# Attention decode with a gated MLP on one core: cross-partition maxima moved to VectorE, paired V accumulators, and output rows as one 512-column product plus a shared remainder

## The chip, the core and the metric

The kernel runs on one core of a Trainium2 chip. The metric is the time of one execution on the device in microseconds (us). The profile is one execution recorded by the hardware. TensorE (PE) multiplies matrices; its weight loads have rows of their own (PEld). VectorE (DVE) does elementwise work and reductions, ScalarE (ACT) does activations and copies, GpSimd (POOL) does elementwise work, and SyncE (SP) issues nearly all large transfers, which one hardware queue carries out in the order of their issue. SBUF is the on-chip memory with 128 partitions, PSUM the accumulators that PE writes. All data are float32, and PE makes two passes for each product, so a product counts twice in the PE rows of a profile. "Order" below means the list of instructions of one engine as the built program holds it; it has no times. PEclk is the share of its full speed that PE was granted.

## The reference

```python
g = sigmoid((x * gate_w).sum(-1))                    # x: [2, 1, 576]
q = x @ wq                                           # [2, 32 heads, 128]
s = q . k_cache * 128**-0.5                          # 2 x 32 heads x 4096 keys
o = softmax(s) @ v_cache                             # [2, 32, 128]
a = o.reshape(2, 1, 4096) @ wo                       # wo: [4096, 576]
h = gelu(x @ w1 + b1)                                # w1: [576, 4608]
b = h @ w2 + b2                                      # w2: [4608, 576]
out = g * a + (1 - g) * b                            # [2, 1, 576]
```

K and V hold 134 MB each (2 x 32 x 4096 x 128 float32); the four weight matrices hold 9.4, 10.6, 10.6 and 9.4 MB (wq, w1, w2, wo). Each is read once.

## The kernel before

**The ring.** Most of SBUF is one tile `ring` with three slots of 64 KB a partition. A slot takes the K or the V of four heads (a unit: 8.39 MB). There are 16 units, so the stream is K0, V0, K1, V1, up to K15, V15, preceded by `wq` and `w1` and followed by three loads named `last` (table `LAST`, line 66): rows 0 to 28 of w2 in the slot of V14, the rest of w2 and wo rows 0 to 16 in the slot of K15, wo rows 16 to 32 in the slot of V15. `load_next` (line 200) issues the next load on SP when the slot's last reader is done: DVE for a K, PE for a V. The last row of wo comes in three pieces, 288, 144 and 144 columns, so that the end has little left to do.

**The start.** The small inputs come over ACT's queue. `xT` (line 273) holds the transposed inputs. `proj` (line 290) makes q and the hidden layer of the MLP from wq and w1, with products that write 32 output partitions each, four side by side. The gate `zps` is a sum of five products (line 281). `q_unit` (line 345) spreads the q of four units over all partitions (tile `q`, two buffers).

**The loop over the units (line 584).** For unit i, `mul` (DVE, line 508) multiplies K in place by q; `red` adds halves on POOL (line 512) and reduces on DVE (lines 513 and 514); `max_p` takes the maximum in each partition; `max_t` turns it with a PE product against the scaled identity `idsc` into PSUM (line 523); `max_n` reduces that on DVE (line 527) in the next turn, before `softmax` (four exponentials on ACT, line 533). `av` (line 540) does 32 products of 512 columns for the unit before, again four side by side on partitions 0, 32, 64 and 96 of a PSUM tile; `keep` (DVE, line 556) masks the tile and `combine` (PE, line 562) adds it into `oall`, once a unit.

**The end (line 604 on).** PE works through the rows of w2 and wo. A row is 576 columns of 128 partitions, and `acc_mm` (line 365) makes two products of 288 columns from it, each with two output partitions; `acc` holds four such groups at partitions 0, 32, 64 and 96, so two rows go side by side. Half of w2's row 35 lies in SBUF as 16 partitions of eight rows (`wx`, function `mlp_x`), read by four small transfers. Rows 0 to 23 of w2 stand ahead of the last `av`; the remaining rows fill the gaps of `norm_sum`, `norm_t` and `o_turn`, which bring the attention output into the layout `oP`. `wo_out(0, FOLD)` adds wo rows 0 to 22. `last_out` (line 445) copies `acc` on ACT, takes wo rows 23 to 31 as four products of 144 columns each (`part`), folds the copied sums in after row 26, and copies the result out in two halves.

The order of each engine is the order in which the code is written (`manual_schedule`).

## Time and profile before

| | before |
|---|---|
| time, median of 3 runs | 721.58 us (721.48 to 721.66) |
| the profiled execution, first to last instruction (span) | 719.80 us |
| difference between the median and the span | 1.78 us |
| mean granted PE clock | 0.663 |
| PE busy | 237.2 us (33%) |
| DVE busy | 516.8 us (72%) |
| transfer engines: share of the span that the queue q1 carried | 99.2% |
| read from memory | 308.59 MB, 429 GB/s |

The profile lists the times of the three runs, but none of its own execution beside its span; the 1.78 us between the two lie outside the first and the last instruction. In rows of the trace in order of time, the first number is the start in us, the second the duration, then come the engine, the line, the operation, out<-in with the shape, the count, and in brackets how long the engine had stood idle and for whom.

### The profile page before, as it was taken

To read this page: it belongs to the slowest core of one execution; us is meant where nothing else is said; L and a number is where in the kernel's file an instruction comes from. 1 tells how busy PE (TensorE), PEld (TensorE's weight loads), DVE (VectorE), ACT (ScalarE), POOL (GpSimd) and SP (SyncE) were. 2 spreads that over 40 slices of the span, in tenths; PEclk is the share of its full clock that TensorE was granted. 3 is DMA by queue.
4 is the path that set the end of the run, shared out by engine and by line. 5 is a ranking of instruction groups with operands and counts; after the bars stand their busy time and mean duration, and the time that the engine had idled before them with its cause. 6 is when DMAs were issued, how large, how long until landed. Compare 5 with 4: busy or idle time off the path is not lost.

```text
span 719.8 us, 3981 instructions
## 1 busy us (share of the span) xinstructions
PE 237.2 (33%) x1695; PEld 72.1 (10%) x1695; DVE 516.8 (72%) x146; ACT 38.3 (5%) x143; POOL 143.8 (20%) x31
## 2 busy tenths in 40 slices
...
GB/s 409 412 443 431 433 441 419 455 416 448 426 444 427 426 438 430 437 430 441 434 433 433 437 427 437 426 437 434 441 430 444 427 437 422 433 441 431 418 425 307
DMA packets 7277, 308.84 MB, mean 429 GB/s; under 512 B 830, under 2 KB 1362, under 8 KB 1628
## 3 DMA queue, kind: packets, MB, share of 16 engines
q1 hardware_dynamic: 7204, 308.55, 99.2%
...
q10 hardware_dynamic: 56, 0.05, 0.0%
...
HBM read 308.59 MB, written 0.00 MB: 429 GB/s over the span
## 4 chain that ended last, share of the span: by engine, by line
DMA 46%; DVE 35%; PE 16%; issue 1%; ACT 1%; ACTq 0%; POOL 0%; DVEq 0%; SPq 0%; POOLq 0%
DMA ring<-in_A_k_cache_dram 41%; DVE ring L508 19%; DVE s L513 10%; PE av L544 8%; DVE s L514 5%; DMA ring<-in_A_wo_dram 3%; DMA ring<-in_gate_w_dram 3%; PE hps L305 2%; PE qps L305 2%; PE oall L562 1%; PE acc L369 1%; PE mt L523 1%; ACT p L533 1%; ACTq L218 0%; DVE m L518 0%
## 5 line engine op out<-in xcount | busy, mean ns | idle before, releaser
L508 DVE TENSOR_TENSOR ring<-ring,q 128x16384 f32<-128x16384 f32 x16 | 275.6, 17225 | 108.9 <-DMA ring<-in_A_k_cache_dram 108.9
L512 POOL TENSOR_TENSOR ring<-ring 128x3968 f32<-128x3968 f32 x16 | 137.0, 8564 | 494.3 <-DVE ring L508 494.3
L513 DVE TENSOR_REDUCE s<-ring 128x66 f32<-128x8448 f32 x16 | 143.2, 8953 | 1.3
L544 PE MATMUL av<-ring,p 128*32 128x512 f32 x1024 | 133.7, 681 | 11.5 <-ACT p L533 6.2
L523 PE MATMUL mt<-idsc,m 128*128 128x128 f32 x32 | 12.6, 498 | 367.5 <-DVE m L518 367.5
L514 DVE TENSOR_REDUCE s<-ring 128x62 f32<-128x3968 f32 x16 | 68.4, 4276 | 0.0
L533 ACT ACTIVATE p<-s,bs 32x128 f32<-32x128 f32 x64 | 25.5, 398 | 487.8 <-DVE bs L527 486.6
L544 PEld LDWEIGHTS av<-ring,p 128*32 128x32 f32 x1024 | 35.6, 124 | 119.3 <-issue 102.4
L523 PEld LDWEIGHTS mt<-idsc,m 128*128 128x128 f32 x32 | 8.0, 310 | 383.2 <-DVE m L518 289.1
L353 PE MATMUL qb<-qm,spread 64*128 64x512 f32 x8 | 8.3, 1138 | 71.2 <-POOL qm L349 71.2
L562 PE MATMUL oall<-avs,pick 128*64 128x512 f32 x32 | 30.6, 1059 | 0.8 <-DVE avs L556 0.8
L556 DVE TENSOR_TENSOR avs<-av,selr 128x512 f32<-128x512 f32 x16 | 10.9, 680 | 16.1 <-PE av L544 16.1
L392 DVE TENSOR_TENSOR ring<-hps,ring 128x384 f32<-128x384 f32 x3 | 1.7, 558 | 27.2 <-PE hps L305 27.0
...
L349 POOL TENSOR_TENSOR qm<-qall,mine 64x512 f32<-64x512 f32 x4 | 4.1, 1032 | 38.4 <-ACT qall L332 38.4
L533 ACT ACTIVATION_READ_ACCUMULATOR p<-s,bs 32x1 f32 x64 | 11.8, 184 | 0.0
L369 PE MATMUL acc<-ring,hg 128*2 128x288 f32 x142 | 11.6, 456 | 0.0
L305 PE MATMUL hps<-ring 128*32 128x384 f32 x120 | 11.5, 549 | 0.0
L305 PE MATMUL qps<-ring 128*32 128x512 f32 x80 | 11.4, 737 | 0.0
L353 PEld LDWEIGHTS qb<-qm,spread 64*128 64x128 f32 x8 | 2.0, 307 | 74.2 <-POOL qm L349 74.2
L479 DVE COPY ring<-res 2x144 f32<-2x144 f32 x1 | 0.3, 298 | 12.6 <-PE res L483 12.6
L272 PE MATMUL xps<-ident,ring 3*128 3x3 f32 x10 | 1.3, 250 | 23.1 <-DMA ring<-in_gate_w_dram 23.1
...
## 6 DMA issues: line engine op xcount, KB each, us to landing
...
```

Of the source, the lines that this page charges most:

```text
L305: nc.tensor.matmul(ps[32 * j:32 * j + 32, :width], lhs, ts[c][:, o:o + width], start=(k == 0), stop=last, skip_group_check=True,)
L353: nc.tensor.matmul(ps, spread, t.rearrange("p u d -> p (u d)"), start=True, stop=True)
L369: nc.tensor.matmul(acc[o:o + m], lhsT, rhs[:, (s - lo) * DS:(s - lo + 1) * DS], start=start, stop=stop, skip_group_check=True)
L508: nc.vector.tensor_mul(kt[i], kt[i], qs[i].unsqueeze(1).to_broadcast([P, R, DH]))
L512: nc.gpsimd.tensor_add(t[:, :, :DH2], t[:, :, :DH2], t[:, :, DH2:])
L513: nc.vector.tensor_reduce(st[i][:, HALVED:], kt[i][:, HALVED:], AX.X, ALU.add)
L514: nc.vector.tensor_reduce(st[i][:, :HALVED], t[:, :, :DH2], AX.X, ALU.add)
L523: nc.tensor.matmul(mt[i], mx[i].to_broadcast([P, P]), idsc, start=True, stop=True)
L533: nc.scalar.activation(p[w, :, e * RB:(e + 1) * RB], st[i][w].rearrange("p (t c) -> p t c", c=RB), AF.Exp, bias=bias[i][w, e:e + 1], scale ...
L544: nc.tensor.matmul(ps[32 * j:32 * j + 32], p[:, EB * t:EB * t + 32], vt[i][:, RB * t:RB * (t + 1)].rearrange("p r d -> p (r d)"), start=(t ...
L556: nc.vector.tensor_mul(t, avs[i].rearrange("p (r d) -> p r d", d=DH), selr.unsqueeze(2).to_broadcast([P, RB, DH]))
L562: nc.tensor.matmul(oall, pick[:, NO - E - i * E:2 * NO - E - i * E], avs[i].rearrange("p r d -> p (r d)"), start=(i == 0), stop=(i == N - ...
```

## The change

1. **Maxima.** `max_t` becomes a DVE transpose of 32 x 32 blocks and `max_n` follows at once on DVE; the product, its PSUM tile and `idsc` go. Each head keeps 32 partitions, so a block is a head. The scale moves into `qall`.
2. **Paired V accumulators.** Two units share one PSUM tile: the even one writes rows 0 to 15 of each group of 32, the odd one rows 16 to 31, by reading the probabilities `p` (now 32 columns apart with zeros between) at two offsets. `keep` and `combine` run once for two units.
3. **Rows of w2 and wo.** `acc_mm` makes one product of 512 columns per row, at partition 32 * (k % 4). The other 64 columns of up to eight rows go into one shared product `acc_rest` into a new PSUM tile `accr`: it multiplies the 16 weight columns of eight rows with the 8 x 64 columns, and only the blocks where row meets row are used. `last_out` picks them on DVE (`sumr`, `sumx`).
4. **w1.** Per chunk of 128 inputs, `proj` makes two banks of 512 columns (eight products) and one product of 512 columns for the remainder, with `xT` padded to 128 columns.
5. **Around it.** `FOLD` moves from 23 to 27; the folding of the sums stands ahead of `part`, not behind its fourth row; `wx` is now half of w2's row 28 and is loaded ahead of w2's rows 28 to 35; `mlp_x` stands between `norm_t` and `o_turn`; the tile `q` has one buffer; the gate is summed on DVE and needs one product.

On PE, between unit 15's sums and the end of its V (before). DMAHW names are counters of transfers, and hg is the hidden layer:

```order
L523 MATMUL mt_1165<-idsc,m_1163 128x128 [waits DVE_49]
L562 MATMUL oall<-avs_1167,pick 64x512 [waits DVE_49]
L369 MATMUL acc<-ring,hg 2x288 [waits DMAHW7_49]
L369 MATMUL acc<-ring,hg 2x288 x27
L369 MATMUL acc<-ring,hg 2x288 [waits DMAHW0_49]
L369 MATMUL acc<-ring,hg 2x288 x19
L544 MATMUL av_1224<-ring,p_114 32x512 [waits PE_49,DMAHW6_49,Activation_49,Pool_49]
L544 MATMUL av_1224<-ring,p_114 32x512 x31
```

The same place now, from the end of V14 on:

```order
L605 MATMUL av_1085<-ring,p_113 32x512 x31
L395 MATMUL acc<-ring,hg 2x512 [waits DMAHW7_49]
L395 MATMUL acc<-ring,hg 2x512 x7
L402 MATMUL accr<-ring,hg 16x512
L395 MATMUL acc<-ring,hg 2x512 x6
L395 MATMUL acc<-ring,hg 2x512 [waits DMAHW0_49]
L395 MATMUL acc<-ring,hg 2x512
L402 MATMUL accr<-ring,hg 16x512
L395 MATMUL acc<-ring,hg 2x512 x8
L402 MATMUL accr<-ring,hg 16x512
L605 MATMUL av_1085<-ring,p_113 32x512 [waits DMAHW6_49,Activation_49,Pool_49]
```

The two products that waited for DVE ahead of w2's first row are gone, so this row now waits for its transfer alone; three shared products stand between the rows.

On PE, from wo's row 16 on (before):

```order
L369 MATMUL acc<-ring,oP 2x288 [waits DMAHW0_49]
L369 MATMUL acc<-ring,oP 2x288 x13
L459 MATMUL res<-ring,oP 2x144 [waits DMAHW1_49]
L459 MATMUL res<-ring,oP 2x144 x15
L469 MATMUL res<-ring,fold 2x144 [waits Activation_49]
L469 MATMUL res<-ring,fold 2x144 x3
L459 MATMUL res<-ring,oP 2x144 [waits DMAHW2_49]
L459 MATMUL res<-ring,oP 2x144 x11
```

And now:

```order
L395 MATMUL acc<-ring,oP 2x512 [waits DMAHW0_49]
L395 MATMUL acc<-ring,oP 2x512 x6
L402 MATMUL accr<-ring,oP 14x448
L395 MATMUL acc<-ring,oP 2x512 [waits DMAHW1_49]
L395 MATMUL acc<-ring,oP 2x512 x3
L402 MATMUL accr<-ring,oP 8x256
L515 MATMUL res<-ring,fold 2x144 [waits Activation_49]
L515 MATMUL res<-ring,fold 2x144
L515 MATMUL res<-ring,fold 2x72 x3
L515 MATMUL res<-ring,fold 2x8
L509 MATMUL res<-ring,oP 2x144 [waits DMAHW2_49]
L509 MATMUL res<-ring,oP 2x144 x11
```

The fold's wait for ACT had sixteen products of wo rows between it and the last row of `acc`; now it has one shared product there, and the last rows of wo stand behind it.

The diff, cut:

```diff
     LAST = (
         (("w2", 0, 14), ("w2", 14, 28)),
-        (("w2", 28, 36), ("wx", 0, 1), ("wo", 0, 8), ("wo", 8, 16)),
+        (("wx", 0, 1), ("w2", 28, 36), ("wo", 0, 8), ("wo", 8, 16)),
         (("wo", 16, 23), ("wo", 23, 27), ("wo", 27, 30), ("wo", 30, 31), ("wo", 31, 32)),
     )
-    FOLD = 23
+    FOLD = 27
...
-    qp = ctx.enter_context(tc.tile_pool(name="qp", bufs=2))
+    qp = ctx.enter_context(tc.tile_pool(name="qp", bufs=1))
...
+    XR = 28
...
+    srcx2 = w2.rearrange("(e c s r) n -> c r e s n", e=XE, c=XC, s=XS)[:, XR, :, :, :DS]
...
+            cut = DS if (w, a) == ("w2", XR) else 0
+            base = first + o - cut
+            for r in range(a, z):
+                place[w, r] = base + (r - a) * D
+                rows[w, r] = ring[:, place[w, r] + (cut if r == a else 0):place[w, r] + D]
+
+            ends = (a * D, a * D + DS, a * D + DS + DO, z * D) if (w, z) == ("wo", 32) else (a * D + cut, z * D)
...
-    idsc = cp.tile([P, P], F32, name="idsc")
-    nc.scalar.mul(idsc, ident, SCALE)
-
...
-        t = cp.tile([P, NT * EB + 32 - EB], F32, name=f"p{j}")
+        t = cp.tile([P, NT * 32 + EB], F32, name=f"p{j}")
...
-    xT = temp(NXT * 32).rearrange("p (c b) -> p c b", b=32)
+    xT = temp(NXT * P).rearrange("p (c b) -> p c b", b=P)
     nc.vector.memset(xT, 0.0)
-    nc.vector.tensor_copy(xT[:, :, :B], xps[:, :, :B])
+    nc.vector.tensor_copy(
+        xT.rearrange("p c (j b) -> p c j b", b=32)[:, :, :, :B], xps[:, :, :B].unsqueeze(2).to_broadcast([P, NXT, NG, B])
+    )
...
-    for c in range(NX + 1):
-        nc.tensor.matmul(zps, gT[:, c:c + 1].to_broadcast([P, P]), xT[:, c, :B], start=(c == 0), stop=(c == NX))
+    gx = temp((NX + 1) * B).rearrange("p (c b) -> p c b", b=B)
+    nc.vector.tensor_mul(gx, xT[:, :NX + 1, :B], gT.unsqueeze(2).to_broadcast([P, NX + 1, B]))
+    gs = temp(B)
+    nc.vector.tensor_reduce(gs, gx.rearrange("p c b -> p b c"), AX.X, ALU.add)
+    nc.tensor.matmul(zps, ones.to_broadcast([P, P]), gs, start=True, stop=True)
...
-
+                if rest is None:
+                    continue
+                lo = len(banks) * width
+                if not last:
+                    cols = ts[c].rearrange("p (r j n) -> p r j n", j=NG, n=group)[:, r, :, lo:]
+                    nc.tensor.matmul(
+                        rest, xT[:, k], cols, start=(k == 0), stop=False,
+                        skip_group_check=True,
+                    )
+                    continue
+                half = NG // 2
+                cols = ts[c].rearrange("p (j n) -> p j n", n=group)[:, :, lo:]
+                for e in range(2):
+                    nc.tensor.matmul(
+                        rest[:, e * half * FC:(e + 1) * half * FC], xT[:, NX + e],
+                        cols, start=False, stop=True, skip_group_check=True,
+                    )
+
...
-    nc.scalar.copy(qall, qps2)
+    nc.scalar.mul(qall, qps2, SCALE)
...
-    acc = ps_acc.tile([P, DS], F32, name="acc")
-
-    def acc_mm(lhsT, rhs, k, start=False, stop=False, lo=0):
+    DM = 512
+    DR = D - DM
+    RM = DM // DR
+    acc = ps_acc.tile([P, DM], F32, name="acc")
+    accr = ps_acc.tile([RM * B, DM], F32, name="accr")
+
+    def acc_mm(lhsT, rhs, k, start=False, lo=0):
         m = lhsT.shape[-1]
-        for s in range(lo, lo + rhs.shape[-1] // DS):
-            o = 64 * (k % 2) + 32 * s
-            nc.tensor.matmul(
-                acc[o:o + m], lhsT, rhs[:, (s - lo) * DS:(s - lo + 1) * DS], start=start, stop=stop, skip_group_check=True
-            )
+        o = 32 * (k % 4)
+        nc.tensor.matmul(
+            acc[o:o + m, lo:lo + rhs.shape[-1]], lhsT, rhs, start=start, stop=False, skip_group_check=True
+        )
+
+    def acc_rest(lhsT, w, a, z):
+        n = z - a
+        rhs = ring[:, place[w, a]:place[w, a] + n * D].rearrange("p (r n) -> p r n", n=D)[:, :, DM:]
+        nc.tensor.matmul(
+            accr[:n * B, :n * DR], lhsT.rearrange("p r b -> p (r b)"), rhs, start=False, stop=False, skip_group_check=True
+        )
...
+    for k in range(4):
+        acc_mm(g1z[:, min(k, 1)], b2r[:, :DM], k, start=True)
+    nc.tensor.matmul(
+        accr, g1z[:, 0, :RM * B], b2r[:, DM:2 * DM], start=True, stop=False, skip_group_check=True
     )
...
+    fold = cp.tile([P, B], F32, name="fold")
+    nc.vector.tensor_reduce(fold, ident.rearrange("p (j c) -> p c j", j=4)[:, :B], AX.X, ALU.add)
+    sixteen = ident[:RM * B, :RM * B].rearrange("p (r b) -> p r b", b=B)
+    diag = cp.tile([RM * B, RM], F32, name="diag")
+    nc.vector.tensor_reduce(diag, sixteen, AX.X, ALU.add)
+    foldr = cp.tile([RM * B, B], F32, name="foldr")
+    nc.vector.tensor_reduce(foldr, sixteen.rearrange("p r b -> p b r"), AX.X, ALU.add)
...
+    hps = [ps_av.tile([P, 512], F32, tag="av", name=f"hps{m}") for m in range(FB)]
+    hrest = ps_sm.tile([P, 512], F32, tag="sm", name="hrest")
+    proj("w1", w1t, hps, hrest)
...
-            acc_mm(hx[:, s], rows["wx"][:, s], s, lo=1)
+            acc_mm(hx[:, s], rows["wx"][:, s], s)
...
-            acc_mm(hg[:, r], rows["w2", r], r)
+            cut = DS if r == XR else 0
+            acc_mm(hg[:, r], rows["w2", r][:, :DM - cut], r, lo=cut)
+        acc_rest(hg[:, lo:hi], "w2", lo, hi)
...
-            acc_mm(oP[:, :, r], rows["wo", r], r)
+            acc_mm(oP[:, r], rows["wo", r][:, :DM], r)
+        acc_rest(oP[:, lo:hi], "wo", lo, hi)
...
-        sums = late(DS)
+        sums = late(DM)
         nc.scalar.copy(sums, acc)
+        sumr = late(DM, RM * B).rearrange("p (r c) -> p r c", r=RM)
+        nc.vector.tensor_mul(
+            sumr, accr.rearrange("p (r c) -> p r c", r=RM), diag.unsqueeze(2).to_broadcast([RM * B, RM, DR])
+        )
+        sumx = late(DR, RM * B)
+        nc.vector.tensor_reduce(sumx, sumr.rearrange("p r c -> p c r"), AX.X, ALU.add)
...
+        def folded(s, o, lhsT, rhs, start=False):
+            nc.tensor.matmul(
+                res[32 * s:32 * s + B, o:o + rhs.shape[-1]], lhsT, rhs, start=start, stop=False, skip_group_check=True
+            )
+
+        for s in range(2):
+            folded(s, 0, fold, sums[:, s * DO:(s + 1) * DO], start=True)
+        H = DO // 2
+        for g in range(2):
+            folded(2 + g, 0, fold, sums[:, DS + g * H:DS + (g + 1) * H], start=True)
+        folded(2, H, fold, sums[:, DS + DO:DS + DO + H])
+        folded(3, H, fold, sums[:, DS + DO + H:])
         for r in range(FOLD, 31):
             for s in range(NC):
                 part(r, s)
-            if r == FOLD + 3:
-                for s in range(NC):
-                    nc.tensor.matmul(
-                        res[32 * s:32 * s + B], fold[:, s // 2], half(sums, s),
-                        start=False, stop=False, skip_group_check=True,
-                    )
+            if r == FOLD + 2:
+                folded(3, DO - DR, foldr, sumx)
...
-        mt[i] = ps_sm.tile([P, P], F32, tag="sm", name=f"mt{i}")
-        nc.tensor.matmul(mt[i], mx[i].to_broadcast([P, P]), idsc, start=True, stop=True)
+        mt[i] = sp.tile([P, PE_], F32, tag="mt", name=f"mt{i}")
+        nc.vector.transpose(mt[i], mx[i].to_broadcast([P, PE_]))
 
     def max_n(i):
-        bias[i] = sp.tile([P, E], F32, tag="bs", name=f"bs{i}")
-        nc.vector.tensor_reduce(bias[i], mt[i].rearrange("o (e p) -> o e p", e=E), AX.X, ALU.max, negate=True)
+        bias[i] = sp.tile([P, 1], F32, tag="bs", name=f"bs{i}")
+        nc.vector.tensor_reduce(bias[i], mt[i], AX.X, ALU.max, negate=True)
...
-        p = pt[i % NPB][:, :NT * EB].rearrange("p (t c) -> p t c", c=EB)
+        p = pt[i % NPB][:, EB:].rearrange("p (t c) -> p t c", c=32)
...
-                bias=bias[i][w, e:e + 1], scale=SCALE, accum_out=rs[w, i * E + e:i * E + e + 1],
+                bias=bias[i][w], accum_out=rs[w, i * E + e:i * E + e + 1],
...
-        ps = ps_av.tile([P, 512], F32, tag="av", name=f"av{i}")
+        half = i % 2
+        if half == 0:
+            avs[i // 2] = ps_av.tile([P, 512], F32, tag="av", name=f"av{i // 2}")
+        ps = avs[i // 2]
...
-                p[:, EB * t:EB * t + 32],
+                p[:, 32 * t + EB * (1 - half):32 * t + EB * (1 - half) + 32],
...
-                start=(t < 4),
-                stop=(t >= NT - 4),
+                start=(half == 0 and t < 4),
+                stop=(half == 1 and t >= NT - 4),
...
-            oall, pick[:, NO - E - i * E:2 * NO - E - i * E], avs[i].rearrange("p r d -> p (r d)"),
-            start=(i == 0), stop=(i == N - 1), skip_group_check=True,
+            oall, pick[:, NO - G - i * G:2 * NO - G - i * G], avs[i].rearrange("p r d -> p (r d)"),
+            start=(i == 0), stop=(i == N // 2 - 1), skip_group_check=True,
...
-            max_n(k)
...
-        if 0 <= k:
-            keep(k)
-            combine(k)
+        max_n(i)
+        if 0 <= k and k % 2:
+            keep(k // 2)
+            combine(k // 2)
 
     k = N - 1
-    max_n(k)
     softmax(k)
-    mlp_out(0, 24)
+    for r in range(0, 24, 8):
+        mlp_out(r, r + 8)
     av(k)
     load_next(("v", k))
     assert not seq
-    keep(k)
-    combine(k)
+    keep(k // 2)
+    combine(k // 2)
...
-    mlp_out(24, 30)
+    mlp_out(24, XR)
     norm_t()
-    mlp_out(30, 33)
+    mlp_x()
     o_turn(turn)
-    mlp_out(33, NF)
-    mlp_x()
-    wo_out(0, FOLD)
+    mlp_out(XR, NF)
+    for a, z in ((0, 8), (8, 16), (16, 23), (23, FOLD)):
+        wo_out(a, z)
     last_out()
```

75 lines of the change are left out of this document (32 added, 43 removed).

## The prediction

> **What bounds the kernel now.** I read the transfer queue and the waits first, then the end in order of time, then the granted clock.
>
> ```profile
> q1 hardware_dynamic: 7204, 308.55, 99.2%
> DVE ring L508 <- DMA ring<-in_A_k_cache_dram: 108.9, 16, 8.0
> 70.19 17.23 DVE L508 TENSOR_TENSOR ring<-ring,q 128x16384 f32<-128x16384 f32 x1 [7.53 <-DMA ring<-in_A_k_cache_dram]
> 651.00 17.22 DVE L508 TENSOR_TENSOR ring<-ring,q 128x16384 f32<-128x16384 f32 x1 [6.63 <-DMA ring<-in_A_k_cache_dram]
> ```
>
> The queue is busy for 99.2% of the span. DVE, the busiest engine, waits for K in each of the 16 units, 6.8 us on average (108.9 / 16). The first and the last multiplication by q start 580.81 us apart, 38.72 us a unit, in which 16.78 MB come in: 433 GB/s, the rate of the whole stream. So the loop is bound by the transfers, and work in it is free as long as a unit has 6.8 us to spare. Outside the stream there are its head and what follows its last byte.
>
> ```profile
> 642.90 0.33 SPq L130 DMA_DIRECT2D ring<-in_A_v_cache_dram  x1
> ring<-in_A_v_cache_dram SPq DMA_DIRECT2D x1, 27.6
> 681.85 0.79 PE L523 MATMUL mt<-idsc,m 128*128 128x128 f32 x2 [26.48 <-DVE m L518]
> 684.47 7.67 PE L369 MATMUL acc<-ring,hg 128*2 128x288 f32 x96
> 689.53 2.05 PEld L369 LDWEIGHTS acc<-ring,hg 128*2 128x2 f32 x40 [0.53 <-DMA ring<-in_B_w_dram]
> 691.96 7.05 PE L544 MATMUL av<-ring,p 128*32 128x512 f32 x64
> 699.82 1.07 PE L562 MATMUL oall<-avs,pick 128*64 128x512 f32 x2 [0.81 <-DVE avs L556]
> 700.89 1.64 PE L369 MATMUL acc<-ring,hg 128*2 128x288 f32 x24
> 702.46 0.27 PE L579 MATMUL oT_t<-ident,ring 64*128 64x64 f32 x1
> 704.09 1.13 PE L369 MATMUL acc<-ring,hg 128*2 128x288 f32 x10
> 707.19 5.99 PE L369 MATMUL acc<-ring,oP 128*2 128x288 f32 x92
> 713.17 0.84 PEld L459 LDWEIGHTS res<-ring,oP 128*2 128x2 f32 x32 [0.56 <-DMA ring<-in_A_wo_dram]
> 713.22 0.40 ACT L448 COPY ring<-acc 128x288 f32<-128x288 f32 x1 [28.13 <-PE acc L369]
> 715.28 0.84 PEld L459 LDWEIGHTS res<-ring,oP 128*2 128x2 f32 x32 [1.02 <-DMA ring<-in_A_wo_dram]
> 716.57 0.10 PEld L459 LDWEIGHTS res<-ring,oP 128*2 128x2 f32 x4 [0.44 <-DMA ring<-in_A_wo_dram]
> 717.71 0.28 SPq L489 DMA_DIRECT2D out_dram<-ring  x1
> ```
>
> In the end PE is behind the transfers until 713.17: it waits for w2's row 14 at 689.53 and then for nothing until wo's row 23. From there it waits for each piece, the last at 716.57, and 3.23 us later the span is over. So the end is set by transfers, but PE has caught up only three waits before it. PE time added after 689.53 first eats 0.56 us at 713.17, then 1.02 and 0.44, and beyond about 2 us it moves the end.
>
> **The price of a product.** Four products on four groups of 32 output partitions run side by side: V's 32 products take 7.05 us, eight rounds of 0.86 us and about 0.17 us of run-out. The 12 of 288 columns take 1.64 us: three rounds of 0.485. The five at 704.09 (the fifth is half a row, alone) take 1.13 us, two rounds: a lone product costs as much as four. The lone 512-column `oall` says the same: 1.07 us, one round and its run-out. All at full clock.
>
> So a row of w2 or wo costs half a round of 288, 0.243 us, and now a quarter round of 512, 0.215 us. But a shared product writes partitions 0 to 15, the group of rows 0, 4, 8: it cannot run beside its successor (row 8, 16 or 24, the same group). Eight rows now cost three rounds, 2.57 us, where they cost 1.94. Half as many instructions, a third more time.
>
> **The sum.** PE's row 0 of w2 now waits only for its transfer. V15 lands at 642.90 + 27.6 = 670.5; 4.13 MB at 433 GB/s need 9.5 us, so rows 0 to 13 can start at 680.0, not 684.47. That is no gain, since row 14 still waits for the second half, at 689.53. From there:
>
> - Rows 14 to 23 with two shared products: rows 14 and 15, shared, 16 to 19, 20 to 23, shared: five rounds, 4.29 us (before 2.43). V15's products start at 693.82, not 691.96 (+1.86).
> - V, `keep`, `combine` and the chain to `o_turn` keep their distance (699.82 - 691.96 = 7.86; 704.09 - 699.82 = 4.27). The fillers fit: four rows and a half-width shared product, 1.29 us, end 2.36 us after the start of `combine`, where `norm_t` starts at 2.64; `mlp_x`, two rounds of 0.485, ends 0.1 us ahead of `o_turn`. PE goes on at 705.95.
> - w2 rows 28 to 35, 2.57; wo rows 0 to 7, 2.57; 8 to 15, 2.57; 16 to 22, 2.47; 23 to 26, 0.86: `acc` is done at 716.99. Before, row 22 was done at 713.18 and rows 23 to 26 needed 1 us more.
>
> ```profile
> L315 ACT COPY ring<-qps 128x512 f32<-128x512 f32 x2 | 1.2, 587 | 10.6 <-PE qps L305 10.6
> L556 DVE TENSOR_TENSOR avs<-av,selr 128x512 f32<-128x512 f32 x16 | 10.9, 680 | 16.1 <-PE av L544 16.1
> L574 DVE TENSOR_REDUCE ring<-oall 64x128 f32<-64x512 f32 x1 | 0.7, 677 | 0.0
> ```
>
> - The new wait: the fold stands ahead of rows 27 to 31 and waits for ACT's copy of 512 columns (0.59, by L315). With 0.22 us of run-out and release ahead and 0.05 behind, the fold starts at 717.85 and takes 0.36 (rounds of 144 and of 72 columns). Behind it wait rows 27 to 29, 0.24 each: 718.94. The fold of the remainder needs the shared product (0.43 after `acc`), the multiplication (0.68, by L556) and the reduction (0.68, by L574): about 719.05, and 0.1 for itself. Row 30: 0.24. Row 31 starts at 719.39. Both DVE prices are from wider tiles, 128 and 64 partitions against 16; were they nothing, row 31 would start 0.2 us sooner, were they double, 1.4 us later; I take them as they are, since the columns are the same 512.
> - From row 31 to the end 3.23 us, unchanged: span 722.62 against 719.80, **+2.82 us**.
>
> **What costs nothing, and its cover.**
>
> ```profile
> L435 DVE STREAM_TRANSPOSE ring<-oT 128x32 f32<-128x32 f32 x2 | 0.3, 192 | 0.0
> 24.68 2.30 PE L281 MATMUL zps<-ring 128*128 128x2 f32 x10 [0.34 <-DVE ring L277]
> 26.91 11.41 PE L305 MATMUL qps<-ring 128*32 128x512 f32 x80
> 44.37 0.33 SPq L130 DMA_DIRECT2D ring<-in_A_k_cache_dram  x1
> 44.81 1.18 PE L369 MATMUL acc<-ring,g1z 1*32 1x288 f32 x8
> 45.92 11.54 PE L305 MATMUL hps<-ring 128*32 128x384 f32 x120
> 54.90 0.33 SPq L130 DMA_DIRECT2D ring<-in_A_v_cache_dram  x1
> 682.26 2.84 SPq L155 DMA_DIRECT2D ring<-in_B_w_dram  x4
> ```
>
> In the loop DVE gains a transpose (0.19 us for 128x32, by the small transposes of the end) and loses every second `keep` of 0.68; either way it has 6.8 us of waiting a unit, and beyond that each us would cost 16. PE loses a product a unit and half the `combine`s, and waits there. The one buffer of `q` makes ACT's copy wait for a multiplication that is over before POOL starts its own part; if not, DVE's spare time covers the copy.
>
> In the head w1 goes from 15 rounds of 384 columns to 15 of 512 (ten of four products, five lone): +3.3 us at 0.64 and 0.86 a round; the biases (1.18 for one round of 288 at half clock) become two rounds of 512, some 2.4 us more; less about 1.3, since four of the gate's five products (2.30) go and about 0.5 of DVE work comes. V0's load then leaves at about 59, not 54.90. It is covered: K0, issued at 44.37, is multiplied at 70.19, so the queue wants V0's issue only by about 66. K0's own issue stands behind `qps` and ACT's small transfers; it goes at 43 to 44 and hides behind w1, so earlier brings nothing, and some 2 us later would open a gap. The wx transfers, 2.8 us of issuing on SP, now stand ahead of w2's rows 28 to 35, while the queue is full until 689.5.
>
> **The clock.**
>
> ```profile
> 39.07:42.48 3.41, 1.16 (x11) 0.91 (x9) 0.00 (x0) 0.26 (x1) 0.76 (x1) 1.00 1.13 487
> 42.48:45.89 3.41, 3.08 (x10) 0.69 (x10) 0.00 (x0) 0.59 (x1) 0.28 (x1) 0.50 0.84 361
> 189.25:192.67 3.42, 1.53 (x16) 0.27 (x8) 3.42 (x1) 0.00 (x0) 0.00 (x0) 1.00 1.02 441
> 192.67:196.08 3.41, 0.00 (x0) 0.00 (x0) 3.41 (x1) 0.00 (x0) 0.00 (x0) 1.00 0.84 365
> 680.77:684.19 3.42, 2.34 (x4) 0.79 (x4) 1.88 (x4) 1.08 (x5) 0.00 (x0) 0.50 0.98 424
> 684.19:687.60 3.41, 3.41 (x29) 0.99 (x32) 0.00 (x0) 0.88 (x4) 0.00 (x0) 0.50 0.90 386
> 687.60:691.01 3.41, 3.41 (x59) 1.22 (x55) 0.00 (x0) 0.00 (x0) 0.00 (x0) 1.00 1.02 440
> 141.47:144.88 3.41, 2.76 (x13) 0.68 (x16) 0.00 (x0) 1.36 (x6) 0.00 (x0) 0.50 0.80 346
> 144.88:148.30 3.42, 3.42 (x39) 1.03 (x32) 0.92 (x1) 0.00 (x0) 0.00 (x0) 1.00 1.22 522
> ```
>
> Behind the bounds of a stretch stands its length, then PE's busy time; the third number from the end is the granted clock. The clock changes on a grid of 3.41 us: after a stretch with 2.76 us of PE work it is full, after 2.34 still half; after 1.16 it falls to half, after 1.53 it stays. Before, PE was busy from 681.85 on and the clock was full from 687.60. Now PE starts at 680.0 on half clock, does five rounds, is done at 684.5 + c/2 (below), between 685.8 and 687.5, and stands idle until 689.53, for 2.0 to 3.7 us. Let the clock rise c after 680.05. A stretch needs about 2.55 us of work for that (between 2.34 and 2.76), so c lies between 2.55 and 5.96, all equally likely. The stretch that follows holds enough work. The next one ends at 686.9 + c and has work from 689.53 on; it has less than about 1.35 us (between 1.16 and 1.53) where c is under 4.0, in 1.45 of 3.41: 4 in 10. Then one stretch runs at half clock, which costs half of it, 1.71 us: span 724.33.
>
> The Trainium skill ("TensorE: Matmul & The Clock Gate", section "HAM oscillation — how this bites in real kernels") has the limit at PE-idle gaps of more than about 3.4 us. By it hardly any phase would fall, and 722.62 would hold nearly always. The stretch at 39.07 fell with at most 2.3 us idle, so the measured row decides.
>
> **Rivals.**
>
> 1. *The clock falls in the gap*: 724.33 as above. For it: the row at 39.07. Against: 6 of 10 phases.
> 2. *Not slower: the shared products run beside the rows.* After 689.53 they cost 0.86 five times and 0.75 once, 5.05 us (the one in the filler and the last, beside ACT's copy, are free); without them `acc` would be done at 711.9 and the transfers would set the end again, span 719.8. For it: nothing but that two products on different groups do overlap. Against: the fifth product at 704.09 and the order, which puts a row of the same group behind each. It decides from 1.4 us hidden on, where the loss goes under 0.2%; at 2.8 nothing is left.
> 3. *The head opens a gap*: K0's issue over 2 us late moves the stream by the excess; at 4 us late about 724.6 with the tail's cost. Against: `qps` starts earlier.
> 4. *Faster*: only by a quicker stream, and its bytes and order are nearly the same; its last pieces are unchanged. About 719 at best.
>
> **How the numbers follow.** A span is 1.78 us short of the runs' median; I keep that. Forecast: 721.58 + 2.82 = 724.40, chance 0.48. Clock falls: 726.11, 0.30. Hidden: 721.6 to 722.5, 0.13. Gap in the head: 726.4 or more, 0.05. Faster: 0.04. A change under 0.2% (1.44 us) is about what a measurement of this kernel cannot tell from none, so slower has 0.83, the same 0.13, faster 0.04. The range runs from 722.4 (nearly all of the shared products' excess hidden) to 726.9 (clock fallen, DVE's picking dearer); the forecast's own range is 723.6 to 725.4.
>
> **What would show it.** The first row of w2 on PE near 680.0; V15's products near 693.8 or, with a fallen clock, 695.5; eight rows and a shared product in 2.6 us; `acc`'s copy near 717.2; PE not waiting for wo any more; K0's and V0's issues near 43 and 59 with the multiplications 38.72 us apart. It is wrong if PE still waits for wo's row 27 or later, if the shared products show less than 0.8 us each, or if the units' pitch has changed.

## The result and the profile after

| | before | after |
|---|---|---|
| time, median | 721.58 us (721.45 to 721.66, 5 runs) | 724.62 us (724.41 to 726.97, 5 runs) |
| ratio, 95% interval | | 1.005 (1.0039 to 1.0061) |
| spans of the runs of after | | 722.3, 722.4, 722.6, 723.9, 724.0 us |

The change costs 3.0 us. The profiled execution of after is the slowest of the five (726.97 us, span 724.0). Of its time 2.97 us lie outside the span, about 1 us more than in the other four (1.98 to 2.2); what that is I didn't find.

First the transfers: the queue on the page of after, and DVE's wait for K in the waits (sum in us, times, longest).

```profile
q1 hardware_dynamic: 7204, 308.55, 98.6%
```

```profile
DVE ring L566 <- DMA ring<-in_A_k_cache_dram: 100.7, 14, 8.9
```

In order of time, the first and the last multiplication by q and the issues of K0 and V0:

```profile
43.12 0.33 SPq L130 DMA_DIRECT2D ring<-in_A_k_cache_dram  x1
59.62 0.33 SPq L130 DMA_DIRECT2D ring<-in_A_v_cache_dram  x1
70.28 17.23 DVE L566 TENSOR_TENSOR ring<-ring,q 128x16384 f32<-128x16384 f32 x1
651.26 17.23 DVE L566 TENSOR_TENSOR ring<-ring,q 128x16384 f32<-128x16384 f32 x1 [6.52 <-DMA ring<-in_A_k_cache_dram]
```

The first and the last multiplication are 580.98 us apart, 38.73 us a unit, where it was 38.72. The head and the loop have moved little: the last multiplication starts 0.26 us later than before, w2's row 14 0.09 us later. The loss lies behind 680. From there, the rows in order of time of the same execution, which answer to the long fence of the prediction:

```profile
680.10 3.57 PE L395 MATMUL acc<-ring,hg 128*2 128x512 f32 x16 [25.03 <-DMA ring<-in_B_w_dram]
689.62 0.60 PE L395 MATMUL acc<-ring,hg 128*2 128x512 f32 x2 [3.38 <-DMA ring<-in_B_w_dram]
694.37 7.43 PE L605 MATMUL av<-ring,p 128*32 128x512 f32 x61
702.63 1.07 PE L622 MATMUL oall<-avs,pick 128*64 128x512 f32 x2 [0.83 <-DVE avs L616]
706.51 0.43 PE L480 MATMUL op_t<-ring 128*128 128x64 f32 x2
706.88 1.47 PE L395 MATMUL acc<-ring,hg 128*2 128x224 f32 x13
708.11 0.59 PE L402 MATMUL accr<-ring,hg 128*16 128x512 f32 x1
710.69 0.59 PE L402 MATMUL accr<-ring,oP 128*16 128x512 f32 x1
713.26 0.59 PE L402 MATMUL accr<-ring,oP 128*16 128x512 f32 x1
715.84 0.54 PE L402 MATMUL accr<-ring,oP 128*14 128x448 f32 x1
717.68 0.59 ACT L492 COPY ring<-acc 128x512 f32<-128x512 f32 x1 [33.01 <-PE acc L395]
718.79 1.03 DVE L498 TENSOR_REDUCE ring<-ring 16x64 f32<-16x512 f32 x1
719.88 0.27 PE L515 MATMUL res<-ring,foldr 16*2 16x64 f32 x2 [0.40 <-DVE ring L498]
721.46 0.29 SPq L547 DMA_DIRECT2D out_dram<-ring  x1
```

PE waits for w2's row 14 at 689.62 and never for wo; before, it had waited there three times. A shared product (L402) comes every 2.57 us, with eight rows between. Behind the last one stand ACT's copy, DVE's picking and the fold of the remainder, and the output leaves at 721.46, before at 717.71.

The same execution in two stretches of the clock's grid (length, then busy time of PE, PEld, DVE, ACT and POOL, then the granted clock, the transfer engines' share and GB/s):

```profile
686.94:690.35 3.41, 0.73 (x8) 0.24 (x11) 0.00 (x0) 0.00 (x0) 0.00 (x0) 1.00 0.94 389
690.35:693.76 3.41, 3.41 (x18) 0.70 (x12) 0.00 (x0) 0.00 (x0) 0.00 (x0) 0.50 0.99 423
```

In the gap ahead of row 14 PE works 0.73 us of a stretch, and the next one runs at half clock. That is rival 1, and it befell this execution. For the other four there are only the spans, by which two runs of five fell.

### The profile page after: what moved, and what is told of

Same layout as the page of the kernel before. It is cut to its first block, busy times and chain, and to the rows that moved or that the text cites. A ratio compares the mean times of both kernels' runs of the same rounds, so it can differ in the third digit from the quotient of the medians.

```text
span 724.0 us, 3595 instructions
## 1 busy us (share of the span) xinstructions
PE 225.8 (31%) x1497; PEld 59.4 (8%) x1497; DVE 518.0 (72%) x163; ACT 38.1 (5%) x142; POOL 145.1 (20%) x32
## 4 chain that ended last, share of the span: by engine, by line
DMA 42%; DVE 36%; PE 19%; ACT 1%; issue 1%; ACTq 0%; POOL 0%; DVEq 0%; SPq 0%; POOLq 0%
DMA ring<-in_A_k_cache_dram 34%; DVE ring L566 19%; PE av L605 10%; DVE s L571 10%; DMA ring<-in_B_w_dram 5%; DVE s L572 5%; DMA ring<-in_gate_w_dram 3%; PE acc L395 2%; PE qps L310 2%; PE hps L310 2%; ACT p L591 1%; PE oall L622 1%; PE accr L402 1%; PE hrest L319 1%; ACTq L218 0%
## 5 line engine op out<-in xcount | busy, mean ns | idle before, releaser
L605 PE MATMUL av<-ring,p 128*32 128x512 f32 x1024 | 140.5, 707 | 165.9 <-ACT p L591 165.9
L622 PE MATMUL oall<-avs,pick 128*64 128x512 f32 x16 | 14.9, 1029 | 197.1 <-DVE avs L616 197.1
L395 PE MATMUL acc<-ring,hg 128*2 128x512 f32 (+1 forms) x72 | 13.5, 778 | 28.4 <-DMA ring<-in_B_w_dram 28.4
L616 DVE TENSOR_TENSOR avs<-av,selr 128x512 f32<-128x512 f32 x8 | 5.5, 684 | 19.4 <-PE av L605 19.4
L622 PEld LDWEIGHTS oall<-avs,pick 128*64 128x64 f32 x16 | 2.2, 196 | 204.4 <-DVE avs L616 204.4
L310 PE MATMUL hps<-ring 128*32 128x512 f32 x80 | 11.3, 691 | 0.0
L395 PE MATMUL acc<-ring,oP 128*2 128x512 f32 x54 | 9.0, 592 | 0.0
```

The source lines that it names most:

```text
L310: nc.tensor.matmul(ps[32 * j:32 * j + 32, :width], lhs, ts[c][:, o:o + width], start=(k == 0), stop=last, skip_group_check=True,)
L395: nc.tensor.matmul(acc[o:o + m, lo:lo + rhs.shape[-1]], lhsT, rhs, start=start, stop=False, skip_group_check=True)
L605: nc.tensor.matmul(ps[32 * j:32 * j + 32], p[:, 32 * t + EB * (1 - half):32 * t + EB * (1 - half) + 32], vt[i][:, RB * t:RB * (t + 1)].rea ...
L622: nc.tensor.matmul(oall, pick[:, NO - G - i * G:2 * NO - G - i * G], avs[i].rearrange("p r d -> p (r d)"), start=(i == 0), stop=(i == N // ...
```

## The experiments

Each is timed beside the kernel before, whose medians were 721.55, 721.60 and 721.56 us in the three sets.

**1. The clock: the changed kernel with the gap filled.**

```diff
         for r in range(lo, hi):
+            if r == 14:
+                idle = ps_sm.tile([P, 512], F32, tag="sm", name="idle")
+                for n in (512, 512, 256):
+                    nc.tensor.matmul(idle[:, :n], ident, rows["w2", 0][:, :n], start=True, stop=True)
```

> The changed kernel with three products added between rows 13 and 14 of w2 (512, 512 and 256 columns into an unused tile, 2.1 us at full clock), where PE otherwise waits for the transfer. Theory 1, the clock falls in that wait in some executions and costs them 1.7 us: no run falls any more, all lie at 724.2 to 725.0. Rival, the two groups of times have another cause: runs at 725.9 to 727 remain, or all are later by the 2.1 us.

Measured: 724.37 us (724.27 to 724.57, 5 runs), ratio 1.0038 (1.0025 to 1.005). Its stretches about row 14:

```profile
688.00:691.41 3.41, 2.87 (x23) 0.92 (x24) 0.00 (x0) 0.00 (x0) 0.00 (x0) 1.00 0.99 422
691.41:694.83 3.42, 3.42 (x37) 0.96 (x34) 0.00 (x0) 0.00 (x0) 0.00 (x0) 1.00 1.01 431
```

The clock stays full and no run stands at 726 any more, so the fallen clock is what parts the spans of the changed kernel's runs. With it gone the change costs 2.82 us. The kernel with the filler is the base of the runs below that leave nothing out.

**2. The groups: shared products beside rows of other groups.**

```diff
+    turn_of, shared = [0], []
...
+        if not start:
+            if shared and turn_of[0] % 4 == 0:
+                shared.pop(0)()
+                turn_of[0] += 1
+            k = turn_of[0]
+            turn_of[0] += 1
         o = 32 * (k % 4)
...
-        acc_rest(hg[:, lo:hi], "w2", lo, hi)
+        shared.append(lambda: acc_rest(hg[:, lo:hi], "w2", lo, hi))
...
-        acc_rest(oP[:, lo:hi], "wo", lo, hi)
+        shared.append(lambda: acc_rest(oP[:, lo:hi], "wo", lo, hi))
...
+    while shared:
+        shared.pop(0)()
```

> The changed kernel, but rows take the four partition groups in turn by a running count, and a shared product goes in where the count comes to group 0, so that it always stands beside three rows. Same products, same arithmetic. Theory 1, it is the group that makes a shared product cost a round: nine products now need 2.25 rounds, PE is done at 712.6 to 714.4, time 721.6 to 722.6. Rival, the shared product is dear in itself (16 columns, pieces of 64 columns read): no gain, 724.4 or more.

Measured: 724.69 us (723.86 to 725.21, 5 runs), ratio 1.0039 (1.0027 to 1.0052): as slow as the changed kernel. Its rows in order of time around and behind `o_turn`:

```profile
701.48 1.07 PE L630 MATMUL oall<-avs,pick 128*64 128x512 f32 x2 [0.83 <-DVE avs L624]
704.55 0.64 PE L403 MATMUL acc<-ring,hx 16*2 16x288 f32 x2
705.12 0.60 PE L410 MATMUL accr<-ring,hg 128*8 128x256 f32 x2
705.65 1.14 PE L403 MATMUL acc<-ring,hx 16*2 16x288 f32 x14
706.72 0.44 PE L488 MATMUL op_t<-ring 128*128 128x64 f32 x2
708.32 0.59 PE L410 MATMUL accr<-ring,hg 128*16 128x512 f32 x1
710.89 0.59 PE L410 MATMUL accr<-ring,oP 128*16 128x512 f32 x1
712.61 0.59 PE L410 MATMUL accr<-ring,oP 128*16 128x512 f32 x1
714.33 0.54 PE L410 MATMUL accr<-ring,oP 128*14 128x448 f32 x1
```

The mechanism holds: from 710.89 on a shared product comes every 1.72 us, two rounds, where it was three. But one slipped in among `mlp_x`'s products (705.12), and `op_t` stands 5.24 us behind `oall`; in the changed kernel it is 3.88. Between these two PE is on the chain that the end waits for, so each round there is paid in full. The gap ahead of row 14 is not filled here, and in this execution the clock fell in it too (granted 0.51 from 689.10 to 692.50), which takes back more of what the rounds had won. So the time of this kernel mixes three things, and the rows, not the median, show the mechanism. The runs also spread over 1.35 us, and the profiled one is the fastest; what parts them I didn't find.

**3. The shared products by themselves: left out.** The kernel leaves out columns 512 to 575 of the rows of w2 and wo.

```diff
-        acc_rest(hg[:, lo:hi], "w2", lo, hi)
...
-        acc_rest(oP[:, lo:hi], "wo", lo, hi)
```

> The changed kernel without the shared products of w2 and wo (left out: in the last 64 output columns all rows of w2 and rows 0 to 26 of wo). Theory 1, each shared product takes a round of its own on PE: without them `acc` is done at 711.5 (full clock) to 713.3 (clock fallen), the transfers set the end again, time 721.5 to 722.1, no run above 722.5. Rival, the fold's wait for ACT and DVE's picking set the end: they stay, so the time stays above 723.

Measured: 722.93 us (722.7 to 723.2, 11 runs), ratio 1.0018 (1.0009 to 1.0027). PE waits for wo once more:

```profile
711.51 1.89 PE L395 MATMUL acc<-ring,oP 128*2 128x512 f32 x14 [0.39 <-DMA ring<-in_A_wo_dram]
714.25 1.04 PE L395 MATMUL acc<-ring,oP 128*2 128x512 f32 x8 [0.85 <-DMA ring<-in_A_wo_dram]
718.77 0.29 SPq L545 DMA_DIRECT2D out_dram<-ring  x1
```

So the shared products are what puts PE behind the transfers. But the time misses the expected 721.5 to 722.1: with the transfers in charge again, 1.4 us are still gone. The trace shows where: wo's row 23 comes at 714.25, before at 713.17, and wo's last packets end at 717.39, before at 716.50; and the closing barrier takes longer. From row 23 on PE's own work leads up to the end, with 0.70 us of waiting for ACT's copy ahead of the fold. Experiments 4 to 7 follow the packets and the barrier.

The gap ahead of row 14 stays unfilled in numbers 3 to 5 and in the second kernel of 6, and in all four profiled executions the clock fell in it (0.50 for one stretch, in number 4 for two). It cost nothing there: PE's weight loads still wait 1.26 to 1.78 us for wo's row 23.

**4. The order of the wx rows** (leaves out the same columns): their four transfers are issued behind w2's rows 28 to 35, as before.

```diff
-                for c in range(XC):
-                    nc.sync.dma_start(xt[c::XC].rearrange("e (s n) -> e s n", s=XS), srcx2[c])
+                xts = [xt]
                 continue
...
+            if (w, a) == ("w2", XR):
+                for c in range(XC):
+                    nc.sync.dma_start(xts[0][c::XC].rearrange("e (s n) -> e s n", s=XS), srcx2[c])
```

> The kernel without the shared products of w2 and wo (it leaves out columns 512 to 575 of those rows; 722.93 us), and with the rows wx issued behind rows 28 to 35 of w2, as in the kernel before, not ahead of them; nothing else. Its place in memory is the same. Theory: issued ahead, the wx rows hold the stream up by 0.6 to 0.9 us to its end (last packets 717.36 there, 716.50 before), and without the shared products TensorE waits for wo's rows (0.39 and 0.85 us), so the time is 722.1 to 722.4 and the last packets stand at 716.4 to 716.6. Rival: the later stream comes from elsewhere (the head, V15's slots), the order of issue costs nothing, as forecast: 722.8 to 723.0.

Measured: 722.95 us (722.82 to 723.22, 11 runs), ratio 1.0019 (1.001 to 1.0028). The order costs nothing; my theory fell. wo's first packet does start 0.7 us sooner (691.26 against 691.97), but the last ones end at 717.19 all the same. The packets show another cause, one of kind "instruction" of 8 KB that neither the kernel before nor the one without the new rows (number 8) has there. The queues from 704 to 708 us, first of this kernel:

```profile
DMA packets 116, 1.65 MB, mean 412 GB/s; under 512 B 10, under 2 KB 10, under 8 KB 10
q1 hardware_dynamic: 115, 1.64, 96.5%
q14 instruction: 1, 0.01, 0.5%
```

In all of the kernels with 197 records of VectorE (drains and semaphores counted) it stands within 0.6 us behind VectorE's record 188, so I take it for VectorE's code; the trace doesn't name the owner. Behind it two packets take longer than their kind: one of 16128 bytes 1.19 us, not 0.60, and one of 9216 bytes 0.84, not 0.35. From 716.80 on, the last packets come in single file, one each 26 ns, as from one engine alone; the others are done by 716.25. By that, the load of code put one of the 16 transfer engines behind. The packets of 9216 bytes are wo's rows 23 to 26, and PE waits for the last of them:

```profile
714.07 0.11 PEld L397 LDWEIGHTS acc<-ring,oP 128*2 128x2 f32 x8 [1.26 <-DMA ring<-in_A_wo_dram]
```

In number 5, without this load, the same wait ends at 713.35.

**5. Four VectorE instructions fewer** (leaves out the same columns and the picking).

```diff
-        nc.vector.tensor_mul(
-            sumr, accr.rearrange("p (r c) -> p r c", r=RM), diag.unsqueeze(2).to_broadcast([RM * B, RM, DR])
-        )
...
-        nc.vector.tensor_reduce(sumx, sumr.rearrange("p r c -> p c r"), AX.X, ALU.add)
...
-    nc.vector.tensor_reduce(diag, sixteen, AX.X, ALU.add)
...
-    nc.vector.tensor_reduce(foldr, sixteen.rearrange("p r b -> p b r"), AX.X, ALU.add)
```

> The run before with the wx rows in their old place (722.95 us; it leaves out columns 512 to 575 of the rows of w2 and wo), and now also without VectorE's picking from accr and the tables for it: four VectorE instructions and one fold fewer, so that VectorE has 193 records, as in the kernel with all parts but the rows, where the last packets came at 716.3. Theory: the kernels with 197 VectorE records all show a load of 8 KB of instruction code right behind VectorE's record 188 (at 704.3 to 706.4 us), on one of the 16 DMA engines; the packets of wo on that engine come late and the last of them alone at 717.1 to 717.2, the others' at 716.2. With 193 records the load stands behind the stream: the last packets at 716.3 to 716.6, and the time 722.2 to 722.5. Rival: the last packets are late for another reason; the load moves, the packets and the time don't: 722.8 to 723.0.

Measured: 722.27 us (722.08 to 722.72, 11 runs), ratio 1.001 (1.0001 to 1.0018). The queues from 704 to 708 us:

```profile
DMA packets 122, 1.75 MB, mean 437 GB/s; under 512 B 10, under 2 KB 10, under 8 KB 10
q1 hardware_dynamic: 122, 1.75, 101.9%
```

The load of code is gone from there, the last packets end at 716.58, and the time is 0.68 us less. In the profiled executions the output leaves 0.90 us sooner (717.64 against 718.54). About 0.7 of that goes with row 23; about 0.2 is the fold of the remainder, which stood on PE's path (716.96 to 717.15 in number 4) and is left out with the picking. DVE's picking itself stood off the path here. The closing barrier takes 0.23 us back: VectorE now pauses in it, 0.47 us between two of its records where in number 4 it was 0.11. Loads of 8 KB between 600 us and the last packet of wo, and the end of that packet, from the traces:

```
kernel                          VectorE records   8 KB loads (us)      last packet (us)
before                          177               633.73, 686.08       716.50
after                           197               686.10, 706.27       717.13
no shared products (3)          197               686.04, 705.20       717.39
wx in its old place (4)         197               686.08, 706.35       717.19
four VectorE instructions fewer 193               686.07               716.58
and GpSimd padded (6)           193               633.92, 686.00       716.37
all parts but the rows (8)      193               686.04               716.33
```

In the other five kernels with 197 VectorE records (1, 2, 9, 10 and the first of 6) the last packet ends at 716.88 to 717.27; in the filled kernel of 8, with 193, at 716.48.

**6. The closing barrier.** Two records of GpSimd in it, start in us and duration in ns:

```
before   719.147 17 EVENT_SEMAPHORE   719.226 17 EVENT_SEMAPHORE
after    722.899 17 EVENT_SEMAPHORE   723.329 17 EVENT_SEMAPHORE
```

0.08 us lie between them before, 0.43 after. The pause stands behind GpSimd's record 68 (counted from the first as 1) in every kernel that has 73 or 74 of them. Six memsets of one element on GpSimd at the start were added twice: to the changed kernel with the gap filled, and to the kernel of number 5.

```diff
     nc.gpsimd.memset(b2r, 0.0)
+    for n in range(6):
+        nc.gpsimd.memset(b2r[:, n:n + 1], 0.0)
```

> The changed kernel with the gap filled (724.37 us), and six memsets of one element each added on GpSimd at the start of the program, which nothing waits for. In the traces GpSimd pauses about 0.4 us ahead of the record with the number 68 in its own stream, whatever the kernel: in the changed kernels that record stands in the closing barrier (GpSimd has 73 or 74 records there), in the kernel before, which has 79, ahead of a sum at 668 that nothing waits for. Theory: the pause belongs to the place in GpSimd's stream, so six more instructions ahead move it out of the barrier: the two GpSimd semaphore records of the barrier stand 0.08 us apart again, and the time is 723.9 to 724.05. Rival: the pause belongs to the barrier or to what the other engines do there: 0.4 us apart still, 724.3 to 724.5.

> The kernel of the run beside it (no shared products, no picking, wx in its old place) with six memsets of one element more on GpSimd at the start, so that GpSimd's own load of code, ahead of its record 68, stands in the stream at 634 and not in the closing barrier. Theory: 0.35 less than the run beside it, 721.8 to 722.15, and with that all but about 0.3 us of what the changed kernel without shared products had lost to the kernel before is found. Rival: the load at 634, like VectorE's at 705, holds one DMA engine up, and what the barrier wins the stream loses: as the run beside it, within 0.1.

Measured: 724.03 us (724.0 to 724.35, 5 runs), 1.0035 (1.0022 to 1.0047), and 721.96 us (721.79 to 722.14, 11 runs), 1.0006 (0.9997 to 1.0014). The two records stand 0.08 us apart in both. The pause has moved into the stream and still stands behind record 68, from 630.01 to 630.44 in the first kernel. An 8 KB load has come into the stream at 633.6 and 633.9, behind GpSimd's record 69; the kernel before has it there too, at 633.73 behind record 68. Each kernel gains 0.3 us. At 633 the load does no harm: the last packets come at 716.37 in the second. So the pause belongs to a place in GpSimd's own stream, and five records fewer had moved it into the barrier, where all engines wait for it. That it is a load of code is inferred: an 8 KB packet follows it, by 3.5 to 4.1 us in the stream and by 1.1 to 1.4 us in the barrier (at 724.03 in the changed kernel, behind the end of its span). The second kernel's output row:

```profile
717.50 0.29 SPq L536 DMA_DIRECT2D out_dram<-ring  x1
```

It leaves 0.2 us sooner than before the change. From there to the end of the span this execution takes 0.3 us more (VectorE pauses in the barrier, 0.47 us between two of its records where before it was 0.11), and 0.1 more lies outside the span: 721.79 us. That this pause too is a load of code was not tried. All five kernels with 193 VectorE records have it in the barrier (0.47 to 0.48 us), and none with 197.

**7. Nothing left out: four small VectorE instructions moved to GpSimd**, in the changed kernel with the gap filled.

```diff
-    nc.vector.memset(pick, 0.0)
+    nc.gpsimd.memset(pick, 0.0)
...
-    nc.vector.memset(g1z, 0.0)
-    nc.vector.tensor_copy(g1z[:, 0, :B], g1[0:1])
+    nc.gpsimd.memset(g1z, 0.0)
+    nc.gpsimd.tensor_copy(g1z[:, 0, :B], g1[0:1])
...
-    nc.vector.memset(xT, 0.0)
+    nc.gpsimd.memset(xT, 0.0)
```

> The changed kernel, nothing left out, with the gap filled (724.37 us) and four small VectorE instructions (three memsets and a copy of two elements) moved to GpSimd: VectorE has 193 records, GpSimd 78, so both loads of code move, VectorE's behind the stream and GpSimd's out of the barrier. Theory: here TensorE and VectorE's picking set the end, not the stream, so the earlier packets (716.3 to 716.6) win nothing, and only the barrier's 0.35 us come back: 723.9 to 724.1. Rival: the late packets held rows 23 to 30 up in the changed kernel too: 723.3 to 723.6.

Measured: 724.17 us (724.06 to 724.89, 5 runs), ratio 1.0038 (1.0025 to 1.005). 0.07 us above the theory's range and far from the rival's: while the shared products are there, the late packets cost nothing. In the profiled execution, the slowest, VectorE's load is gone from 704 to 706, and GpSimd's pause stands in the stream with an 8 KB load behind it (672.62). The last packet ends at 717.03, which looks late. But this execution was 0.69 us late before that load: its last multiplication by q starts at 651.88, with the gap filled alone at 651.19. Less that, the last packet stands at 716.34, as expected. In the barrier GpSimd no longer pauses, but VectorE does, for 0.47 us, so less than the expected 0.35 us comes back.

**8. All parts but the rows of w2 and wo**, which are as before, first plain, then with the gap filled by four products of 512 columns.

```diff
-    FOLD = 27
+    FOLD = 23
...
-        acc_rest(hg[:, lo:hi], "w2", lo, hi)
...
+        for s in range(lo, lo + rhs.shape[-1] // DS):
+            o = 64 * (k % 2) + 32 * s
```

> The changed kernel with w2 and wo as before (two products of 288 a row, fold and order as before): the maxima on DVE, the paired V accumulators, the nine products of w1 and the gate stay. Theory 1, all this is covered by the transfers: 721.4 to 722.0. Rival, the loop or the head has its part in the loss: 722.5 or more.

> All parts of the change but the rows (722.5 us before, its runs in two groups, 722.2 to 722.95 and 723.5 to 723.75), with four products of 512 columns, whose result nothing reads, between w2's rows 13 and 14, where TensorE stood idle for 4.4 us and its clock fell for 3.3 us. Theory: the upper group is the runs in which the clock stays down longer; with the clock at full speed throughout there is one group, 722.0 to 722.4, about as the lower one, since 0.3 us of slack lies behind TensorE there. Rival: the groups have another reason and stay, with a median of 722.5 and runs above 723.4.

Measured: 722.5 us (722.2 to 723.75, 11 runs, four of them above 723.4), 1.0019 (1.001 to 1.0028), and 722.2 us (721.99 to 722.61, 11 runs), 1.0009 (1.0 to 1.0018). The stretches about row 14, plain and filled:

```profile
686.59:690.00 3.41, 0.53 (x9) 0.22 (x13) 0.00 (x0) 0.00 (x0) 0.00 (x0) 0.99 0.92 393
690.00:693.33 3.33, 3.33 (x32) 1.18 (x28) 0.00 (x0) 0.00 (x0) 0.00 (x0) 0.50 1.00 420
```

```profile
686.59:690.00 3.41, 3.02 (x14) 0.99 (x17) 0.00 (x0) 0.00 (x0) 0.00 (x0) 1.00 0.96 411
690.00:693.33 3.33, 3.33 (x52) 1.33 (x48) 0.00 (x0) 0.00 (x0) 0.00 (x0) 1.00 0.99 415
```

Dropping the maxima from PE lets w2 start 4.5 us sooner, and all that it brings here is a gap in which the clock falls. The profiled execution of the plain kernel was of the lower group, though its clock fell too; why four runs lose another 1.2 us I saw in no trace, only that none of eleven does once the gap is filled. Filled, the output leaves at 717.60, 0.1 us sooner than before: maxima, paired accumulators, w1 and gate cost nothing in the work; the 0.6 us are in the barrier and outside the span.

**9. The fold behind rows 27 to 29**, in the changed kernel with the gap filled.

```diff
-        for s in range(2):
-            folded(s, 0, fold, sums[:, s * DO:(s + 1) * DO], start=True)
...
+            if r == FOLD + 2:
+                for s in range(2):
+                    folded(s, 0, fold, sums[:, s * DO:(s + 1) * DO])
...
+            if r == FOLD + 3:
                 folded(3, DO - DR, foldr, sumx)
```

> The changed kernel with the gap before row 14 of w2 filled (as in the run before, 724.37 us) and, beside that, the fold of acc moved behind row 29 and that of the shared products behind row 30, so that TensorE no longer stands still for ScalarE's copy of acc ahead of rows 27 to 29. Theory: VectorE's picking (its product at 718.08, its sum over 1.03 us until 719.82 in the changed kernel's trace) is what the end waits for, not the copy, so only row 30 (0.2 to 0.25 us), which now stands ahead of the second fold, is won: 724.0 to 724.2. Rival: the copy is what the end waits for; then the 0.6 us between the last product and the fold and row 30 come back together: 723.4 to 723.7.

Measured: 724.16 us (723.83 to 724.43, 5 runs), ratio 1.0036 (1.0022 to 1.005). Its end in order of time:

```profile
715.90 0.59 ACT L496 COPY ring<-acc 128x512 f32<-128x512 f32 x1 [31.52 <-PE acc L395]
717.02 1.01 DVE L502 TENSOR_REDUCE ring<-ring 16x64 f32<-16x512 f32 x1
718.08 0.27 PE L519 MATMUL res<-ring,foldr 16*2 16x64 f32 x2 [0.60 <-DVE ring L502]
```

PE does rows 27 to 30 during the copy and then waits for DVE. The new wait of the fold cost nothing: the rival's 723.4 to 723.7 is excluded. The 0.2 us won are what the theory gave for row 30, but the runs of the two kernels overlap (723.83 to 724.43 and 724.27 to 724.57), so that size is not shown.

**10. All mends together**, nothing left out: 2 with no shared product between `norm_sum` and `o_turn`, 4, 1, 9 and the memsets of 6.

```diff
+            if shared and turn_of[0] % 4 == 0 and not hold[0]:
...
+    hold[0] = True
     mlp_out(24, XR)
     norm_t()
     mlp_x()
     o_turn(turn)
+    hold[0] = False
```

> The changed kernel with all five mends: the group of a product by a running count, with shared products issued where three rows stand beside them and none between norm_sum and o_turn; the rows wx issued behind rows 28 to 35 of w2, as before; the gap filled; the fold behind row 29; six memsets on GpSimd. Theory: with ten rounds where the changed kernel has thirteen, TensorE is behind the last product of acc at about 714 to 714.5, VectorE's picking ends by 716.3, and the last transfers (716.5 in the kernel before) set the end again: 721.4 to 722.0. Rival: a chain that these traces don't show beside one another (V15's combination to o_turn, the fold behind the copy) is late all the same: 722.3 to 723.5.

Measured: 723.18 us (723.06 to 723.26, 11 runs), ratio 1.0022 (1.0013 to 1.003): the rival. It is 1.2 us better than the changed kernel with the gap filled, and still slower than before. Two stretches of the clock's grid:

```profile
686.85:690.27 3.42, 1.43 (x11) 0.40 (x13) 0.00 (x0) 0.00 (x0) 0.00 (x0) 1.00 0.93 398
690.27:693.68 3.41, 3.41 (x20) 0.75 (x15) 0.00 (x0) 0.00 (x0) 0.00 (x0) 0.50 1.01 423
```

The waits for w2 and wo in order of time, and the fold of the remainder:

```profile
689.66 2.16 PE L407 MATMUL acc<-ring,hg 128*2 128x512 f32 x9 [1.99 <-DMA ring<-in_B_w_dram]
713.99 0.09 PEld L407 LDWEIGHTS acc<-ring,oP 128*2 128x2 f32 x4 [0.96 <-DMA ring<-in_A_wo_dram]
716.04 0.23 PEld L525 LDWEIGHTS res<-ring,oP 128*2 128x2 f32 x12 [1.11 <-DMA ring<-in_A_wo_dram]
717.75 0.27 PE L531 MATMUL res<-ring,foldr 16*2 16x64 f32 x2 [0.31 <-DVE ring L514]
```

Since the rows end a round earlier the filler is over too soon, and the clock falls with 1.43 us of work in the stretch. Even so PE waits for wo again (0.96 and 1.11 us on its weight loads). wo is late as in number 4, with an 8 KB load at 705.08 and the last packets at 717.13. What the end waits for is DVE's picking (717.75): it starts behind the last products of `acc`, and these begin with row 23, which comes at 713.99, before at 713.17. So the fallen clock is not what sets this execution's end. Taking four VectorE instructions off this kernel as well was not tried; by number 6 it would bring VectorE's pause into the barrier.

## Why the prediction was right

The forecast, +2.82 us with the clock at full speed, is what the kernel with the gap filled shows: 724.37 against 721.55. And the changed kernel itself, at 724.62, lies between that and the case of rival 1. Term by term, in the executions of the changed kernel (clock fallen) and of the one with the gap filled (clock full):

- **What sets the end.** Right. The transfers bind the loop, the head is covered (issues at 43.12 and 59.62, forecast 43 to 44 and 59), and behind row 14 PE falls back behind the transfers for good (with the clock full, weight loads wait once more, 0.21 us at 714.14). Left out, the shared products give the waits for wo back (3). The wx order, costed at nothing, cost nothing where it was tried, without the shared products (4).
- **The price of a product.** Right: eight rows and a shared product take 2.57 to 2.58 us, three rounds, because it stands in the group of its successor. Put beside other groups it is two, 1.72 us (2).
- **Rows 14 to 23, five rounds, 4.29 us.** One round too many. Rows 14 and 15 stand in groups 2 and 3 and run beside the first shared product, in group 0. `oall` starts at 700.94 with the clock full, forecast 693.82 + 7.86 = 701.68: 0.74 too late, although row 14 came 0.09 later than forecast.
- **w2 rows 28 to 35.** 0.48 us too dear: row 28's product is only 224 columns wide and leaves group 0 early. The rows take 1.23 us to their shared product (706.88 to 708.11), not two rounds, 1.71.
- **DVE's picking.** Too cheap: the sum takes 1.03 us, not 0.68. The row that I took reads PSUM and adds four values to each of 128, this one reads SBUF and adds eight to each of 64; which of these makes it dearer is open. It, not ACT's copy, is what the end waits for (9). From the last product of `acc` to the fold of the remainder this makes 0.36 us more than forecast.
- **From row 31 to the end, 3.23 us, unchanged.** Too short: 718.75 to 722.37 are 3.62 with the clock full. 0.33 of the 0.39 is GpSimd's pause in the barrier (0.41 us between the two records instead of 0.08; 6), which I had not thought of.
- **The sum.** With the clock full, w2's row 28 starts at 705.30, forecast 705.95: -0.65, as 0.09 of the 0.74 is lost again up to `o_turn`. Rows 28 to 35 add -0.48, the picking +0.36, the fold of the remainder with row 30 +0.11 (718.30 to 718.75, forecast 0.34), and the end +0.39. The span is 722.37, not 722.62. Outside the span lie 1.90 us, not 1.78. That the total came out within 0.1 us is luck in this measure: terms that were wrong by 0.4 to 0.7 us cancel.
- **The clock.** Right in kind. By the spans two runs of five fell, forecast 4 in 10, and the fall cost 1.3 to 1.7 us of span, forecast 1.71; five runs are few for the odds. By the rule of the Trainium skill that I set against it ("TensorE: Matmul & The Clock Gate", section "HAM oscillation — how this bites in real kernels": gaps over about 3.4 us) this gap of 3.38 us is at the limit and decides nothing. But experiment 10 shows a fall after a gap of 1.99 us, and there the trace disagrees. My own limit, between 1.16 and 1.53 us of work in a stretch, is not sharp either: experiment 10 fell after 1.43 us, and the changed kernel kept its clock after 1.43 us:

```profile
536.75:540.16 3.41, 1.43 (x16) 0.22 (x8) 3.41 (x1) 0.00 (x0) 0.00 (x0) 1.00 0.93 404
540.16:543.57 3.41, 0.00 (x0) 0.00 (x0) 3.41 (x1) 0.00 (x0) 0.00 (x0) 1.00 1.11 480
```

- **Rival 2**, that the shared products run beside the rows, was false for the order as written, but for the first shared product behind row 14. It was the right idea of a mend, yet hiding them did not bring it under 0.2%: at 723.18 other things had taken over (10). The shared products with their picking cost about 724.37 - 722.27 = 2.1 us (1 against 5); this is an estimate, since the two kernels also differ in the filled gap, the place of wx and VectorE's load.
